# Normalising on two engines instead of three, new prices in the planner, one copy for the third bank of turned weights

## The chip, the core and the metric

The kernel runs on one core of a Trainium2 chip. The metric is the device time of one execution in microseconds, as the median of the runs shown. TensorE does the matrix products and the transposes; VectorE (DVE), ScalarE (ACT) and GpSimd (POOL) move results out of the PSUM banks, split numbers into high and low parts, and do the softmax; SyncE (SP) issues the DMAs. All arithmetic is in float32, and products are made from high and low parts in a rounded format (`fp32r`), so that one product of the reference is three matmuls.

## The reference

Three parts follow each other. Attention over 4 batches and 12 heads of 448 x 64; a feed-forward net with a gating convolution; and an attention with 4 experts, of which each row takes its best two.

```python
scores = scale * q @ k.T                      # (4, 12, 448, 448), causal
attn = exp(scores - max) / (sum + 1e-9)
x = attn @ v                                  # -> (4, 448, 768)

h = maximum(x @ w_in, 0.0)                    # 768 -> 1024
conv_out = sum over k of conv_w[k] * hp[:, k:k + S]   # 3 taps along the sequence
x = h * sigmoid(conv_out) @ w_out             # 1024 -> 768

topk = the two largest of x @ w_gate
for e in range(4):
    q, k, v = x @ wq[e], x @ wk[e], x @ wv[e] # 768 -> 64 each
    a = causal softmax of scale * q @ k.T
    ye = a @ v @ wo[e]                        # 64 -> 768
    out += weight of e (0 where not chosen) * ye
```

## The kernel before

Two heads, or two experts, make a **pair**: one takes the lower 64 partitions and the other the upper. There are 24 pairs of heads (6 in each batch) and 8 pairs of experts (2 in each batch), and all 32 go through the same steps. `scores` (L683) makes the causal scores of a pair, 24 matmuls into four banks (L734), DVE takes the masked maximum while copying them out (L711, tile `e`, with the maxima in `stat`), and ACT does the exponential with its sum (L715). `norms` (L748) adds the sums (L753), takes the reciprocal (L755) and multiplies the ten pieces of `e` with it: L760 on ACT, L763 on DVE or POOL. The pieces have 64, 192, 320 or 384 columns (four, two, two and two of them in a pair). For expert pairs L763 multiplies with the gate `coef` as well, and there ACT doesn't take part. `weigh` (L783) turns the weights: 14 transposes (L781) into banks, whose contents are copied into the tile `z` (by the helper `high`, L670 on ACT, L672 on DVE, L674 on POOL), and eight matmuls with the values (`rest`, L814). The first bank of transposes gives four small copies of 128 columns, two banks give one copy of 512 each, and the third gives two copies of 256. A subtraction (helper `low`, L678) gives the low part of a split number, on DVE or POOL.

The FFN works in eight slices of 128 of the 1024 columns: the weights are loaded and, in batch 0, split into tiles `slab` (`split_in`, L902); L966 makes the products; L984 is the ReLU on ACT, L990 to L1003 the convolution, L1010 the tanh. L885 to L889 are the rounding of numbers by integer steps in `single`. `output` (L1134) multiplies with the experts' output weights, copies a bank of 128 x 448 to the tile `work` and writes it out (L1155).

Nothing runs in the order of the text. Each step is recorded in `Plan` with the engines that may do it, a price for each, its inputs and outputs; `Plan.run` ranks the steps by how much work hangs on them, `schedule` hands each engine the ready step of the highest rank at the planned time, and then everything is written out in the order of planned starts. The prices are formulas (`scale_cost` for normalising, `psum_cost` for copies out of a bank, `LAG` for the time from the end of a step on one engine to the start of one that reads it on another), `SHIFTS` is a table that nudges ranks, and `FILLS` (30) idle products (L1160) may stand where TensorE has nothing to do. An engine executes its steps in the written order, and waits on semaphores for data. The choice of an engine for each step is the plan's too. So a step that takes longer than its price makes whatever was planned behind it late, and what stands behind that on the same engine.

## Time and profile before

| | us |
|---|---|
| median of 3 runs | 534.32 |
| lowest and highest | 533.75, 536.55 |
| the profiled execution | 535.11 |
| its span, first to last instruction | 533.3 |
| PE busy | 515.4 |
| DVE busy | 421.6 |
| ACT busy | 357.7 |
| POOL busy | 112.0 |

The profile comes from one execution. Its span leaves out some 2 us around the first and the last instruction. "Busy" is the time in which an instruction of that engine runs; waits are idle time in front of an instruction, and the profile names the instruction that ended them (the releaser). A line of a helper, like L670 or L678, stands for many different steps, which are told apart by the tiles that they read and write. PEclk is the granted clock of TensorE as a share of full speed.

### The profile page before, as it was taken

How to read it: one execution, taken by the hardware profiler on the slowest of the kernel's cores; microseconds unless marked ns; L12 is line 12 of the kernel's file. 1: busy time of each engine (PE TensorE's matmuls, PEld its weight loads, DVE VectorE, ACT ScalarE, POOL GpSimd, SP SyncE). 2: the span in 40 equal slices, each digit the busy share in tenths (PEclk: the TensorE clock that was granted, in tenths of full speed). 3: DMA queues.
4: the chain of work that ended last, by engine and by line, in shares of the span. 5: the costliest groups of instructions: out<-in, count | busy, mean ns of one | idle time of the engine just before them, and what ended most of it. 6: DMA issues, size and time to landing. Idle time of an engine off the chain costs nothing.

```text
span 533.3 us, 10436 instructions
## 1 busy us (share of the span) xinstructions
PE 515.4 (97%) x3554; PEld 436.2 (82%) x3556; DVE 421.6 (79%) x1300; ACT 357.7 (67%) x1058; POOL 112.0 (21%) x132
## 2 busy tenths in 40 slices
PE   8799999899899999899999999999999999999997
PEld 4678888778689898798898777998987778989875
DVE  6999599889798549999259999986389999842581
ACT  2876279789986557686249986755488867732572
POOL 3152017334232021160012511101114000000010
PEclk9999999899989999999999999999999999999999
DMA  9984246845587011374201573763003315610042
GB/s 239 256 222 135 63 149 195 255 120 206 167 246 201 23 36 37 139 250 163 68 2 46 146 219 84 249 215 87 1 1 113 117 49 194 221 59 1 10 154 104
DMA packets 63381, 69.92 MB, mean 131 GB/s; under 512 B 36576, under 2 KB 57312, under 8 KB 63328
## 3 DMA queue, kind: packets, MB, share of 16 engines
q1 hardware_dynamic: 63328, 69.26, 42.7%
q8 instruction: 28, 0.46, 0.4%
q14 instruction: 25, 0.20, 0.1%
HBM read 55.87 MB, written 13.37 MB: 130 GB/s over the span
## 4 chain that ended last, share of the span: by engine, by line
PE 47%; DVE 25%; ACT 8%; issue 2%; ACTq 0%; DVEq 0%
PE pf L966 34%; DVE e L711 7%; DVE e L763 5%; PE bank L814 5%; DVE z L672 4%; PE bank L781 3%; ACT e L715 3%; PE bank L734 3%; ACT e L760 2%; DVE pair L678 1%; DVE pair L672 1%; DVE work L995 1%; PE bank L966 1%; ACT z L670 1%; PE pf L1074 1%
## 5 line engine op out<-in xcount | busy, mean ns | idle before, releaser
L966 PE MATMUL pf<-pair,slab 128*128 128x448 f32 (+2 forms) x984 | 218.5, 368 | 4.3 <-ACT hp L984 2.7
L966 PEld LDWEIGHTS pf<-pair,slab 128*128 128x128 f32 x984 | 171.8, 189 | 22.2 <-ACT hp L984 3.7
L715 ACT ACTIVATE e<-e,stat 128x192 f32<-128x192 f32 (+3 forms) x256 | 127.1, 499 | 23.8 <-DVE stat L711 23.4
L711 DVE CUSTOM_DVE_ANT_0 e<-bank,mask 128x448 f32<-128x448 f32 (+3 forms) x256 | 92.1, 414 | 6.7 <-PE bank L734 6.5
L966 PE MATMUL pf<-pair,wqks 128*128 128x448 f32 x384 | 81.1, 369 | 0.0
L966 PEld LDWEIGHTS pf<-pair,wqks 128*128 128x128 f32 x384 | 71.4, 188 | 7.0 <-ACT pair L670 0.3
L781 PE MATMUL bank<-ident,e 128*128 128x128 f32 x448 | 70.7, 280 | 6.4 <-DVE stat L711 3.5
L678 POOL TENSOR_TENSOR pair<-work,pair 128x448 fp32r<-128x448 f32 (+1 forms) x39 | 48.6, 1260 | 105.6 <-PE bank L734 39.1
L781 PEld LDWEIGHTS bank<-ident,e 128*128 128x128 f32 x448 | 52.7, 142 | 16.9 <-DVE stat L711 3.6
L672 DVE COPY z<-bank 64x128 f32<-64x128 f32 (+2 forms) x121 | 48.7, 429 | 20.9 <-PE bank L781 16.7
L670 ACT ACTIVATE z<-bank 64x128 f32<-64x128 f32 (+2 forms) x135 | 45.8, 367 | 13.4 <-PE bank L814 7.4
L760 ACT ACTIVATE e<-e,stat 64x64 f32<-64x64 f32 (+3 forms) x116 | 49.4, 454 | 7.5 <-DVE stat L755 5.9
L734 PE MATMUL bank<-pair,pair 64*128 64x448 f32 (+3 forms) x576 | 49.6, 291 | 0.1
L814 PE MATMUL bank<-z,block 128*64 128x448 f32 (+3 forms) x384 | 48.7, 395 | 0.0
L715 ACT ACTIVATION_READ_ACCUMULATOR e<-e,stat 128x1 f32 (+1 forms) x256 | 48.5, 189 | 0.0
L995 DVE SCALAR_TENSOR_TENSOR work<-hp,cws,work 128x448 f32<-128x448 f32 x64 | 43.7, 694 | 3.9 <-ACT work L990 3.3
L734 PEld LDWEIGHTS bank<-pair,pair 64*128 64x128 f32 (+1 forms) x576 | 41.9, 172 | 3.3 <-issue 1.6
L814 PEld LDWEIGHTS bank<-z,block 128*64 128x64 f32 x384 | 27.3, 139 | 20.6 <-issue 11.5
L966 PE MATMUL pf<-wvs,pair 128*128 128x260 f32 x288 | 37.3, 286 | 0.0
L678 DVE TENSOR_TENSOR pair<-pf,pair 64x448 fp32r<-64x448 f32 (+1 forms) x24 | 15.0, 623 | 26.7 <-ACT pair L670 26.4
L966 PEld LDWEIGHTS pf<-wvs,pair 128*128 128x128 f32 x288 | 35.5, 188 | 0.3
L670 ACT ACTIVATE pair<-pf 64x448 fp32r<-64x448 f32 (+1 forms) x24 | 12.8, 541 | 32.3 <-PE pf L966 32.0
(99 smaller groups left out, 593.7 us busy)
## 6 DMA issues: line engine op xcount, KB each, us to landing
slab<-w_scratch SPq DMA_DIRECT2D x24, 768.0 KB, 4.6
work<-in_w_out SPq DMA_DIRECT2D x8, 768.0 KB, 4.8
work<-in_w_in SPq DMA_DIRECT2D x8, 768.0 KB, 5.7
w_scratch<-slab SPq DMA_DIRECT2D x8, 768.0 KB, 4.5
work<-in_qk SPq DMA_DIRECT2D x48, 112.0 KB, 3.4
work<-in_qk SPq DMA_DIRECT2D x24, 224.0 KB, 4.3
out<-work SPq DMA_DIRECT2D x24, 224.0 KB, 2.1
slab<-wo_scratch SPq DMA_DIRECT2D x6, 768.0 KB, 4.3
```

The costliest lines, as they stand in the source:

```text
L670: nc.scalar.activation(dst(), src(), AF.Copy)
L672: nc.vector.tensor_copy(dst(), src())
L678: return lambda e: engine(e).tensor_sub(dst(), src(), f32(h()))
L711: nc.vector.tensor_tensor_reduce(out=ec(o, c), in0=bank(o, c), in1=m, scale=-0.125, scalar=3.0e38, op0=OP.add, op1=OP.min, accum_out=st[ro ...
L715: nc.scalar.activation(ec(o, c), ec(o, c), AF.Exp, bias=st[rows, 0, o, c:c + 1], scale=-1.0, accum_out=st[rows, 1, o, c:c + 1])
L734: nc.tensor.matmul(bank(o, c), q(s)[own, Q0[c]:Q0[c] + QN[c]], k(t)[own, kc(o, c)], start=i == 0, stop=i == 2)
L760: nc.scalar.activation(dst(), src(), AF.Copy, scale=st[rows, 3, o, c:c + 1])
L763: engine(en).tensor_scalar(dst(), src(), st[rows, 3, o, c:c + 1], gate, op0=OP.mult, op1=OP.mult)
L781: P.op({"T": TURN}, lambda _: nc.tensor.transpose(dst(), src(), ident[:, :]), r=r, w=keys)
L814: nc.tensor.matmul(ps[own, S - n:S], v(k, o), z[:, 1024 * o + n0:1024 * o + n0 + n], start=k == 0, stop=k == 3)
L966: nc.tensor.matmul(out_ap(), a(), b(), start=first, stop=end), r=r, w=[(ps, 0)])
L995: return lambda _: nc.vector.scalar_tensor_tensor(cv[:, :S], hp[:, i:S + i], cws[:, fc, i:i + 1], cv[:, :S], op0=OP.mult, op1=OP.add)
```

## The change

1. Prices: normalising costs 0.053 us more on ACT, 0.05 on DVE, 0.055 on POOL; a copy of up to 128 columns out of a bank 0.065 more (0.12 below 64 columns); the lag between two steps on ACT is 0.15 instead of 0. The price of one FFN step on ACT is written out, so that it stays as it was.
2. `NORM` lets ACT and DVE normalise the pairs of heads, and DVE alone those of experts. POOL no longer does.
3. The third bank of transposes is copied in one step, which needs all four transposes. For that the columns of `z` are laid out in another order (`KEYS`).
4. The very last output is copied and written in two halves of 224 columns.
5. `SHIFTS` is another table (its rows tell nothing and are left out), and the plan comes out in another order.

```diff
-KEYS = ((0, 448), (448, 320), (832, 192), (768, 64))
+KEYS = ((0, 448), (704, 320), (512, 192), (448, 64))
...
 SHIFTS = (
-    (-1, 3596, 3648, -2), (15400, 386, 426, 0.5), (30038, 244, 284, 1), (-1, 4324, 4325, 0.5), (-1, 4323, 4324, 0.5),
+    (52200, 289, 299, 0.5), (-1, 4336, 4337, 2), (-1, 4333, 4334, -2), (-1, 4333, 4334, 2), (-1, 4331, 4332, -2),
...
-    LAG = {"TT": 0.0, "TA": 0.2, "TV": 0.2, "TG": 0.27, "TD": 0.19, "AT": 0.23, "AA": 0.0, "AV": 0.16, "AG": 0.17, "AD": 0.14,
+    LAG = {"TT": 0.0, "TA": 0.2, "TV": 0.2, "TG": 0.27, "TD": 0.19, "AT": 0.23, "AA": 0.15, "AV": 0.16, "AG": 0.17, "AD": 0.14,
...
+NORM = ("AV", "V")
...
 def scale_cost(n, on="AVG"):
-    return only(on, {"A": on_scalar(n) + 0.137, "V": on_vector2(n) + 0.065, "G": 0.245 + n * 0.000835})
+    return only(on, {"A": on_scalar(n) + 0.19, "V": on_vector2(n) + 0.115, "G": 0.3 + n * 0.000835})
...
 def psum_cost(n, on="A"):
-    return dict(only(on, {"A": on_scalar(n), "V": on_vector(n)}))
+    more = 0.12 if n < 64 else 0.065 if n <= 128 else 0.0
+    return dict(only(on, {"A": on_scalar(n) + more, "V": on_vector(n) + more}))
...
-            P.op(scale_cost(n, "VG" if moe else "AVG"), fn, r=r + [(st, "r")] + ([(COEF, b)] if moe else []), w=w)
+            P.op(scale_cost(n, NORM[moe]), fn, r=r + [(st, "r")] + ([(COEF, b)] if moe else []), w=w)
...
-            for o in range(2):
-                P.op(psum_cost(256, "AV"), high(lambda o=o: spread(z, 2048, 1024 * o + 64, 832, 128),
-                                                lambda t=t, o=o: t[:, 256 * o:256 * o + 256].rearrange("p (b c) -> p b c", b=2)),
-                     r=[(t, 2 * o), (t, 2 * o + 1)], w=[(z, (o, 3))])
+            P.op(psum_cost(512, "AV"), high(lambda: z[:, :].rearrange("p (a b) -> p a b", a=4)[:, :, 64:192],
+                                            lambda t=t: t[:, :].rearrange("p (a b) -> p a b", a=4)), r=[(t, j) for j in range(4)], w=[(z, 3)])
...
-        P.op({"T": 4 * 960 / 2400 + 0.23}, rest, r=[(z, (o, i)) for o in range(2) for i in range(4)] + v_r, w=[(ps, 0)], mode=2)
+        P.op({"T": 4 * 960 / 2400 + 0.23}, rest, r=[(z, (o, i)) for o in range(2) for i in range(3)] + [(z, 3)] + v_r, w=[(ps, 0)], mode=2)
...
-            P.op(scale_cost(S, "A"), c1, r=[(hp, 0), (CWS, 0)], w=[(cv, 0)])
+            P.op({"A": on_scalar(S) + 0.137}, c1, r=[(hp, 0), (CWS, 0)], w=[(cv, 0)])
...
-            P.op(psum_cost(S, "AV"), high(lambda o=o: o[:, :S], lambda ps=ps: ps[:, :S]), r=[(ps, 0)], w=[(o, 0)])
-            P.op(dma_cost(229376, 1792), lambda _, dc=dc, o=o: nc.sync.dma_start(out[b, dc], o[:, :S]), r=[(o, 0)])
+            parts = 1 + (b + 1 == B and dc + 1 == NK)
+            for i in range(parts):
+                own = slice(i * S // parts, (i + 1) * S // parts)
+                P.op(psum_cost(S // parts, "AV"), high(lambda o=o, own=own: o[:, own], lambda ps=ps, own=own: ps[:, own]), r=[(ps, 0)], w=[(o, i)])
+                P.op(dma_cost(229376 // parts, 1792 // parts), lambda _, dc=dc, o=o, own=own: nc.sync.dma_start(out[b, dc][:, own], o[:, own]), r=[(o, i)])
```

The instructions of each engine, counted in both programs: TensorE 3,338 in both, of the same kinds; DVE 1,302 before and 1,315 after; ACT 804 and 808; POOL 137 and 91; SP 264 and 265. The lines of the changed kernel are 16 to 19 higher than those of before (L763 is L781, L670 is L688, L678 is L696).

Three places of the order follow. The first is POOL in the middle of the program, around the first pairs of experts of batch 0 (`e_123`, `e_124`: the tiles of two such pairs; `pair`: a tile for a high or low part). Before:

```order
L678 TENSOR_TENSOR pair_139<-work_150,pair_136 128x448
L674 TENSOR_SCALAR pair_141<-work_150 128x896
L678 TENSOR_TENSOR pair_143<-work_150,pair_141 128x448 x2
L763 TENSOR_SCALAR e_123<-e_123,stat_86,coef 128x320
L763 TENSOR_SCALAR e_123<-e_123,stat_86,coef 128x192
L763 TENSOR_SCALAR e_123<-e_123,stat_86,coef 64x64
L763 TENSOR_SCALAR e_123<-e_123,stat_86,coef 128x384 x2
L763 TENSOR_SCALAR e_124<-e_124,stat_87,coef 64x64 x2
L674 TENSOR_SCALAR gx_146<-pair_138 128x128
```

The same pair on DVE after the change, whose POOL has no such step:

```order
L690 COPY z_114<-bank_157 128x4x128
L771 TENSOR_REDUCE stat_86<-stat_86 128x8
L773 RECIPROCAL stat_86<-stat_86 128x8
L781 TENSOR_SCALAR e_123<-e_123,stat_86,coef 128x320
L781 TENSOR_SCALAR e_123<-e_123,stat_86,coef 128x192 x2
L781 TENSOR_SCALAR e_123<-e_123,stat_86,coef 64x64 x2
L781 TENSOR_SCALAR e_123<-e_123,stat_86,coef 128x320
L781 TENSOR_SCALAR e_123<-e_123,stat_86,coef 64x64 x2
L781 TENSOR_SCALAR e_123<-e_123,stat_86,coef 128x384 x2
L696 TENSOR_TENSOR pair_131<-bank_156,pair_131 128x448
```

All ten pieces of this pair stand on DVE in one row now, where POOL had five of them.

The second place is ACT ahead of a ReLU (`hp`) of the FFN of batch 0, with the pieces of one pair of heads (`e_125`), turned weights (`z`) and a slab. Before:

```order
L760 ACTIVATE e_125<-e_125,stat_88 128x384
L1010 ACTIVATE work_150<-work_150 128x448
L670 ACTIVATE z_114<-bank_153 64x2x64
L670 ACTIVATE z_114<-bank_153 64x128
L670 ACTIVATE pair_142<-bank_155 128x448
L670 ACTIVATE z_114<-bank_153 64x128
L670 ACTIVATE z_114<-bank_157 128x2x256
L670 ACTIVATE z_114<-bank_153 64x2x64
L670 ACTIVATE z_114<-bank_156 128x2x256
L670 ACTIVATE slab_149<-work_150 128x768
L1010 ACTIVATE work_150<-work_150 128x448
L984 ACTIVATE hp_96<-pf_152 128x448
```

And the rows ahead of a ReLU of the same batch after the change:

```order
L778 ACTIVATE e_124<-e_124,stat_87 128x320
L778 ACTIVATE e_124<-e_124,stat_87 64x64 x2
L688 ACTIVATE z_114<-bank_158 128x4x128
L778 ACTIVATE e_124<-e_124,stat_87 128x192 x2
L778 ACTIVATE e_124<-e_124,stat_87 64x64 x2
L778 ACTIVATE e_124<-e_124,stat_87 128x384
L1026 ACTIVATE work_150<-work_150 128x448 x2
L733 ACTIVATE e_125,stat_88<-e_125,stat_88 128x448
L688 ACTIVATE pair_142<-work_150 128x896
L1000 ACTIVATE hp_95<-pf_152 128x448
```

The small copies out of a bank and the slab that stood ahead of the ReLU are elsewhere, and an exponential and a long pair copy stand there.

The third place is the end of DVE's program, with the last two pairs of experts (`e_123`, `e_124`). Before:

```order
L672 COPY work_150<-pf_151 128x448
L763 TENSOR_SCALAR e_123<-e_123,stat_86,coef 128x192
L763 TENSOR_SCALAR e_123<-e_123,stat_86,coef 64x64 x3
L763 TENSOR_SCALAR e_123<-e_123,stat_86,coef 128x384 x2
L753 TENSOR_REDUCE stat_87<-stat_87 128x8
```

After:

```order
L781 TENSOR_SCALAR e_123<-e_123,stat_87,coef 128x320
L781 TENSOR_SCALAR e_123<-e_123,stat_87,coef 64x64 x2
L781 TENSOR_SCALAR e_123<-e_123,stat_87,coef 128x320
L781 TENSOR_SCALAR e_123<-e_123,stat_87,coef 64x64 x2
L781 TENSOR_SCALAR e_123<-e_123,stat_87,coef 128x384
L771 TENSOR_REDUCE stat_88<-stat_88 128x8
L781 TENSOR_SCALAR e_123<-e_123,stat_87,coef 128x384
```

Before, the other four pieces of `e_123` were POOL's; now the last pair but one is wholly on DVE, two pieces of it further ahead than these rows.

## Rows read from the trace of the kernel before

**Rows 1.** The page, part 1: busy us (share of the span) xinstructions of each engine.
```profile
PE 515.4 (97%) x3554; PEld 436.2 (82%) x3556; DVE 421.6 (79%) x1300; ACT 357.7 (67%) x1058; POOL 112.0 (21%) x132
```

**Rows 2.** The page, part 4: shares of the span in the chain that ended last.
```profile
PE 47%; DVE 25%; ACT 8%; issue 2%; ACTq 0%; DVEq 0%
```

**Rows 3.** Busy by stage: us of PE, PEld, DVE, ACT, POOL; PEclk, DMA share, GB/s.
```profile
91.00:116.00 25.00, 23.39 (x178) 18.84 (x176) 21.42 (x68) 20.12 (x67) 10.38 (x11) 0.93 0.74 210
...
116.00:138.00 22.00, 21.06 (x133) 18.31 (x131) 20.39 (x52) 20.80 (x58) 9.60 (x8) 1.00 0.51 180
...
138.00:162.00 24.00, 22.18 (x135) 18.88 (x132) 21.50 (x45) 20.68 (x53) 5.11 (x7) 0.93 0.68 211
...
202.00:225.00 23.00, 21.62 (x180) 17.98 (x179) 22.06 (x75) 15.41 (x53) 3.05 (x5) 1.00 0.25 83
...
286.00:329.00 43.00, 41.81 (x350) 32.78 (x348) 40.64 (x166) 37.09 (x123) 13.54 (x17) 1.00 0.50 140
...
389.00:454.00 65.00, 63.46 (x493) 51.92 (x492) 61.62 (x224) 51.95 (x172) 10.31 (x15) 1.00 0.31 102
...
sum 533.30, PE 515.40 PEld 436.20 DVE 421.62 ACT 357.66 POOL 112.00; mean PE 36.81 PEld 31.16 DVE 30.12 ACT 25.55 POOL 8.00
```

**Rows 4.** The same view, two us at a time, behind two waits of TensorE.
```profile
102.00:104.00 2.00, 2.00 (x9) 1.91 (x10) 1.83 (x6) 0.95 (x2) 1.44 (x2) 0.51 1.01 366
...
104.00:106.00 2.00, 2.00 (x10) 1.75 (x9) 1.00 (x6) 2.00 (x8) 0.00 (x0) 0.63 1.09 214
...
146.00:148.00 2.00, 1.99 (x8) 1.08 (x9) 1.94 (x4) 1.97 (x5) 0.00 (x0) 0.61 0.64 259
...
148.00:150.00 2.00, 2.00 (x13) 1.73 (x10) 2.00 (x4) 1.50 (x6) 0.00 (x0) 0.54 0.64 191
```

**Rows 5.** Timeline, expert pairs: start us, us, engine line op tiles xcount [idle <-releaser].
```profile
211.79 3.15 POOL L763 TENSOR_SCALAR e<-e,stat,coef 128x320 f32<-128x320 f32 x5 [18.30 <-PE bank L781]
...
212.69 2.64 DVE L763 TENSOR_SCALAR e<-e,stat,coef 64x64 f32<-64x64 f32 x4
...
217.16 1.14 PE L781 MATMUL bank<-ident,e 128*128 128x128 f32 x8 [1.38 <-DVE stat L711]
...
435.71 3.13 DVE L763 TENSOR_SCALAR e<-e,stat,coef 128x320 f32<-128x320 f32 x9
```

**Rows 6.** The timeline around 97 to 102 us, DVE, POOL and PE.
```profile
97.48 3.22 DVE L763 TENSOR_SCALAR e<-e,stat 128x192 f32<-128x192 f32 x6
...
97.74 2.05 POOL L678 TENSOR_TENSOR slab<-work,slab 128x768 fp32r<-128x768 f32 x1 [0.29 <-ACT slab L670]
...
101.95 1.28 PE L781 MATMUL bank<-ident,e 128*128 128x128 f32 x5 [1.57 <-DVE pair L678]
```

**Rows 7.** The timeline around 136 to 145 us, ACT and PE.
```profile
135.94 4.07 ACT L760 ACTIVATE e<-e,stat 128x192 f32<-128x192 f32 x9
...
144.87 0.47 PE L966 MATMUL pf<-pair,slab 128*128 128x448 f32 x1 [1.80 <-ACT hp L984]
```

**Rows 8.** Groups of instructions, normalising: busy us, mean ns of one, idle before.
```profile
L763 DVE TENSOR_SCALAR e<-e,stat 64x64 f32<-64x64 f32 (+3 forms) x82 | 29.5, 387 | 1.7 <-ACT e L760 0.4
...
L763 DVE TENSOR_SCALAR e<-e,stat,coef 64x64 f32<-64x64 f32 (+3 forms) x69 | 24.8, 400 | 0.8
...
L763 POOL TENSOR_SCALAR e<-e,stat 64x64 f32<-64x64 f32 (+3 forms) x42 | 21.3, 516 | 61.4 <-DVE stat L755 34.1 <-ACT work L670 11.0 <-DVE e L763 7.5
...
L763 POOL TENSOR_SCALAR e<-e,stat,coef 64x64 f32<-64x64 f32 (+3 forms) x11 | 9.9, 904 | 67.6 <-ACT e L715 37.5 <-PE bank L781 18.3 <-DVE e L763 11.6
```

**Rows 9.** The same groups by form, copies of turned weights out of a bank.
```profile
L672 DVE COPY z<-bank 128x256 f32<-128x256 f32 x30 | 11.4, 413 | 5.5 <-PE bank L781 5.5
...
L672 DVE COPY z<-bank 128x512 f32<-128x512 f32 x34 | 22.8, 683 | 10.1 <-PE bank L781 6.4 <-PE bank L814 3.3
...
L670 ACT ACTIVATE z<-bank 128x256 f32<-128x256 f32 x34 | 11.7, 379 | 2.6 <-PE bank L781 2.3
```

**Rows 10.** The timeline at the end, ACT's last copy.
```profile
529.86 0.55 ACT L670 ACTIVATE work<-bank 128x448 f32<-128x448 f32 x1 [0.48 <-PE bank L966]
```

## What the change will do to the time

> **What bounds the kernel now.** I read the profile from the outside in. First the busy times: TensorE is busy for 97% of the span, DVE for 79%, ACT for 67%, POOL for 21% [rows 1]. The reader is to see that the time can fall only where TensorE waits or runs at its lower clock, since the change leaves its 3,338 instructions (matmuls, weight loads and the rest) the same in kind and number. Then the chain that ended last: it is 47% PE and 25% DVE [rows 2], so in a quarter of the span the releaser of TensorE's work is a queue of DVE. Then the busy time by stage, which says where the waits are [rows 3]: TensorE is busy 515.40 of 533.30 us, and of the 17.9 us in which it is idle 1.6 lie in 91 to 116, 0.9 in 116 to 138, 1.8 in 138 to 162, 1.4 in 202 to 225, 1.2 in 286 to 329 and 1.5 in 389 to 454; the stages left out between them have next to none, the two ends the rest. In two of these stages the granted clock is 0.93. [...]
>
> What makes these waits? The order was planned from prices, and where an engine takes longer than its price, TensorE arrives before its data. At 211.79 POOL normalises five pieces in 3.15 us, and beside it DVE takes 2.64 us for four small ones of 64x64 with the gate [rows 5]; undisturbed, nine of all sizes take 3.13 us at 435.71, 0.35 each [rows 5]. The old price of a 64x64 piece on DVE is 0.068 + 64/1920 + 0.065 = 0.17 us, four cost 0.7: DVE comes out 1.9 us late, and TensorE then waits 1.38 us for the masked maximum behind it. At 97.48 the same: six pieces take 3.22 us, 0.54 each, beside a subtraction of 2.05 us on POOL; TensorE waits 1.57 us at 101.95 for DVE [rows 6]. At 144.87 it waits 1.80 us for ACT's ReLU. ACT is late there without POOL: its nine pieces take 4.07 us [rows 7], where the old prices (0.187 + n/1200: 0.240, 0.347, 0.454 and 0.507 for 64, 192, 320 and 384, of which there are three, two, two and two) give 3.34.
>
> **The change, part by part.** *Prices.* The new ones add 0.053 to each piece on ACT and 0.05 on DVE, and 0.065 to each copy of up to 128 columns out of a bank: the nine pieces are now priced 3.81, and a 64x64 piece on DVE 0.22. They move towards the rows but do not reach them. A right price saves nothing by itself; it lets the plan put products in front of the work that would wait.
>
> *Normalising.* POOL loses 42 pieces without gate at 0.516 and 11 with gate at 0.904, 31 us; DVE gets 29 and 11 more, ACT 13 [rows 8]. On DVE's own rows (29.5 + 24.8 us for 151 pieces, 0.36 each) that is +14.4 us; on ACT, by the nine in 4.07, 0.45 each, +5.9. Against it stands what POOL cost DVE: 2.64 where four undisturbed pieces take 1.4, so 1.2 at this one place [rows 5], and 3.22 for 2.1, so 1.1, at the other [rows 6]; but there the neighbour is a subtraction, which POOL keeps (35 of this form become 31, six of slab form become four). At 211.6 the pair took DVE and POOL together until 215.3. All ten on DVE last 10 x 0.35 = 3.5 us and the copy of 0.68 us stands among them: 215.8, not earlier. So the gain is not that DVE is done sooner but that the plan knows when it is.
>
> [...]
>
> *Third bank.* DVE's 30 copies of 256 columns at 0.413 become 5 of 512 at 0.683: 12.4 - 3.4 = 9.0 us less [rows 9]. ACT's 34 at 0.379 become 27 longer ones; with DVE's ratio of the two kinds, 0.63 each, that is 4 us more for ACT, an estimate. The price of one copy is that the first half can't start after two transposes. Two more transposes are 0.5 us at most later (eight at 217.16 last 1.14, so 0.14 each, plus whatever product stands between), but one copy of 0.68 is shorter than two of 0.41 behind each other by 0.15: between -0.15 and +0.5 for the products that read it, hidden where other products stand in front. I take nothing, because in the order scores or products stand between the last transposes and the weighted sum in 25 of the 32 pairs before and in 24 now.
>
> *Other moves.* DVE also takes four more subtractions of pairs, two of slabs, two casts of slabs, and gives five z copies and some pair casts to ACT: with the above DVE gets +8.4 us in all by the trace's mean durations, ACT about +6, POOL loses about 31. Spread over 533 us DVE stays under 81%; what counts is where it falls. In the last pair before the end DVE gets four pieces more, 4 x 0.36 = 1.4 us [rows 8], and POOL's 2.3 us beside it go; seven idle products instead of three stand there in the order, and some 1.2 us of further products before the transposes. I take +0.3, from 0 to +1.4.
>
> *Last output in halves.* The last copy takes 0.55 us and starts at 529.86 [rows 10]; its transfer of 224 KB follows. Two copies of half length take at least 0.55 together, and by the mean of 0.379 for 256 columns on ACT [rows 9] about 0.75. So the second half is issued up to 0.2 later, behind the first, and carries half the bytes. Between -0.3 and +0.3, I take 0, as both copies are on the same engine.
>
> *New order.* Here lies the gain, place by place. At 217.16 the plan's error was 1.9 us and is now 10 x 0.35 less the new prices (four of 0.22, two each of 0.28, 0.35 and 0.38, 2.9) = 0.6: I take 1.1 of the 1.38 (0 to 1.4). At 101.95 the subtraction of POOL stays possible, so I take half of 3.3, 1.6 (0 to 3.3). At 144.87 ACT was late by 0.73 on the nine pieces, of which the new prices find 0.48, and the ten or so small z copies and the lag between ACT's own instructions (0 becomes 0.15) are priced now too: half of 3.5, 1.75 (0 to 3.5). The other middle waits (0.94 at 116 to 138, 1.5 at 389 to 454, about 1.2 between 286 and 329, 3.7 in all) have DVE or ACT as releaser too; by the same half, 1.8 (0 to 3.7). The added DVE load takes something back, where DVE has no room: it is busy 21.42 of 25 us, 20.39 of 22 and 61.62 of 65 in the stages around these waits [rows 3], a fifth of the kernel, and a fifth of 8.4 is 1.7 us (0 to 5).
>
> The sum: -1.1 - 1.6 - 1.75 - 1.8 + 1.7 + 0.3 = -4.3 us on the profiled 535.11, so 530.9. The profiled run lies 0.8 above the median of 534.32; against the median this is 530.0.
>
> **The rivals.** *No change.* The plan moves its mistakes elsewhere: the waits come back in other places because DVE now does what POOL did, and the 8.4 us arrive where it is the releaser (25% of the chain: 2.1 us), a new wait of 2 us eating the rest: 534. For it: prices that are still too low by about 0.05 a piece on 342 pieces. Against it: the two deepest waits have known causes that were repriced. [...]
>
> *Slower, by DVE between 91 and 138.* DVE is busy there 41.8 of 47 us, 5.2 to spare. In the new order one more pair of the second batch is normalised and copied in this stretch, beside the splitting of the FFN's weights. Its DVE work is 3.5 us at least (ten pieces); priced over all rows of both orders the 60 us of TensorE's work around it hold 59.6 us of DVE's before and 67.0 now, an estimate of 7.4 more. [...] It decides from 5.2 us of added work there. Against it: the same stretch loses POOL's interference, 1.1 us in the one case seen, and part of the added work stands behind products.
>
> *Everything goes.* Both deep waits vanish with their clock and the others with them: 1.4 + 3.3 + 3.5 + 3.7 = 11.9 less 1.5 of losses, 524.
>
> **How the numbers follow.** Forecast 0.42, everything goes 0.15, no change 0.24, slower 0.19. What a measurement here can tell is about 0.5%, 2.7 us: faster is under 531.6, slower over 537.0. The forecast's own range is 527 to 532.5, so a little of it is within 0.5%, and so is a little of the slower case: faster 0.55, same 0.29, slower 0.16. For 8 in 10 the range takes in the better part of the quick case, down to 524, and of the slow one, up to 538. The predicted time is 530.
>
> **What would show it.** The steps are right if in the profile after POOL is near 80 us and DVE near 425 or a little below 430 (+8.4 on 421.6, less some 4 us of interference, by the two places of 1.1 and 1.2), if PE's idle time falls from 17.9 to about 14, if the granted clock has at most one fall, and if the mean of DVE's normalising falls below 0.36. The third bank is right if the eight products behind it wait no more than before. The forecast is wrong if a new long wait of TensorE stands between 90 and 140 with DVE as releaser and a clock below 1 behind it; if PE's idle time falls but the time does not, the lower clock has taken the gain; and if the waits vanish by themselves at places whose engines were not repriced, the order did it and not the prices.

## The result and the profile after

The changed kernel takes 529.52 us (median of 6 runs, 528.43 to 531.82) against 535.06 for the kernel before (6 runs, 533.75 to 536.55): a ratio of 0.9902, with a 95% interval of 0.9874 to 0.993, so 3.7 to 6.7 us less. A second set of runs (**after_again** below, 12 beside 17 of the kernel before) gave 529.19 and 0.9927 (0.99 to 0.9953). The profiled execution took 528.43 us, with a span of 526.6.

The page's part 1 (busy us, share of the span, instructions) and part 4 (shares of the chain that ended last) of the changed kernel, against [rows 1] and [rows 2]:

```profile
PE 511.0 (97%) x3556; PEld 433.6 (82%) x3556; DVE 425.6 (81%) x1313; ACT 357.7 (68%) x1062; POOL 86.6 (16%) x86
...
PE 66%; DVE 27%; DMA 3%; ACT 2%; issue 1%; SPq 0%; ACTq 0%; DVEq 0%
```

TensorE's idle time, span less busy, goes from 533.3 - 515.4 = 17.9 us to 526.6 - 511.0 = 15.6. Its busy time goes down by 4.4 us as well, with the same matmuls. The two stretches of lower clock in the profile of before [rows 4] come to 1.7 + 1.7 = 3.4 us of that, and the stages below have none. So of 6.7 us between the two spans 2.3 are waits and 4.4 are busy time, most of it clock.

Busy time by stage of the changed kernel (us of PE, PEld, DVE, ACT, POOL; PEclk; DMA share; GB/s), against [rows 3]:

```profile
90.00:115.00 25.00, 24.90 (x216) 19.75 (x212) 24.14 (x73) 19.24 (x62) 6.32 (x6) 1.00 0.69 198
115.00:140.00 25.00, 23.89 (x153) 19.62 (x154) 24.94 (x62) 23.07 (x63) 8.59 (x5) 1.00 0.59 193
140.00:165.00 25.00, 24.58 (x154) 20.68 (x152) 24.67 (x71) 24.11 (x78) 13.54 (x15) 1.00 0.87 247
165.00:200.00 35.00, 33.17 (x253) 29.52 (x252) 21.48 (x68) 17.14 (x52) 3.08 (x3) 1.00 0.11 27
200.00:230.00 30.00, 30.00 (x195) 26.18 (x190) 27.09 (x88) 20.74 (x60) 2.15 (x3) 1.00 0.45 145
...
285.00:325.00 40.00, 38.29 (x326) 30.43 (x323) 38.85 (x147) 33.59 (x111) 9.79 (x9) 1.00 0.51 138
...
385.00:450.00 65.00, 64.39 (x504) 53.30 (x503) 58.62 (x213) 51.25 (x165) 8.51 (x10) 1.00 0.32 103
...
sum 526.60, PE 511.01 PEld 433.56 DVE 425.63 ACT 357.68 POOL 86.65; mean PE 36.50 PEld 30.97 DVE 30.40 ACT 25.55 POOL 6.19
```

The last stage of each kernel, first before, then after:

```profile
514.00:533.30 19.30, 14.81 (x88) 10.82 (x87) 6.10 (x15) 7.75 (x21) 0.00 (x0) 0.97 0.40 137
```

```profile
508.00:526.60 18.60, 15.16 (x94) 11.43 (x92) 6.24 (x15) 7.49 (x19) 0.00 (x0) 1.00 0.43 140
```

And normalising on DVE in the changed kernel, against [rows 8] (xcount | busy us, mean ns of one | idle before):

```profile
L781 DVE TENSOR_SCALAR e<-e,stat 64x64 f32<-64x64 f32 (+3 forms) x111 | 37.1, 373 | 1.4 <-ACT e L778 0.3
...
L781 DVE TENSOR_SCALAR e<-e,stat,coef 64x64 f32<-64x64 f32 (+3 forms) x80 | 27.6, 381 | 0.8
```

The three places of the prediction are empty of waits: nothing stands for 101.95 and 144.87, and the stage of the expert pairs, 200 to 230, has none. A wait of 0.99 us for ACT's ReLU at 127.98 is much like the one of 0.94 before (116 to 138 in [rows 3]). DVE is busy for 73.75 of the 75 us between 90 and 165. TensorE's longest wait in the middle stands right behind that, and it is new (timeline of the changed kernel: start us, us, engine, line, op, tiles, idle before and its releaser):

```profile
163.69 2.85 POOL L696 TENSOR_TENSOR pair<-work,pair 128x448 fp32r<-128x448 f32 x2
164.00 1.55 DVE L1019 SCALAR_TENSOR_TENSOR work<-work,hp 128x448 f32<-128x448 f32 x1
...
165.59 1.20 DVE L690 CAST pair<-work 128x448 fp32r<-128x448 f32 x1
...
166.84 1.49 PE L982 MATMUL pf<-pair,wqks 128*128 128x448 f32 x6 [1.83 <-DVE pair L690]
```

Two instructions of DVE last 1.55 and 1.20 us beside two subtractions of POOL. The same forms mostly take 0.62 and 0.39. The two subtractions suffer too: 2.85 us together, where two take 2.25 elsewhere (311.95, below).

### The profile page after: what moved, and what is told of

Same layout as the page of the kernel before. It is cut to its first block, busy times and chain, and to the rows that moved or that the text cites. A ratio compares the mean times of both kernels' runs of the same rounds, so it can differ in the third digit from the quotient of the medians.

```text
span 526.6 us, 10385 instructions
## 1 busy us (share of the span) xinstructions
PE 511.0 (97%) x3556; PEld 433.6 (82%) x3556; DVE 425.6 (81%) x1313; ACT 357.7 (68%) x1062; POOL 86.6 (16%) x86
## 4 chain that ended last, share of the span: by engine, by line
PE 66%; DVE 27%; DMA 3%; ACT 2%; issue 1%; SPq 0%; ACTq 0%; DVEq 0%
PE pf L982 45%; DVE e L729 7%; PE bank L830 6%; PE bank L799 6%; PE bank L752 6%; DVE e L781 5%; DVE pair L696 3%; DVE z L690 3%; DVE work L1011 2%; DMA block<-in_vv 2%; DVE pair L690 1%; PE pf L1179 1%; DMA work<-in_qk 1%; PE bank L982 1%; DVE work L905 1%
## 5 line engine op out<-in xcount | busy, mean ns | idle before, releaser
L733 ACT ACTIVATE e<-e,stat 128x320 f32<-128x320 f32 (+3 forms) x256 | 126.9, 499 | 21.4 <-DVE stat L729 20.9
L729 DVE CUSTOM_DVE_ANT_0 e<-bank,mask 64x64 f32<-64x64 f32 (+3 forms) x256 | 93.0, 413 | 14.8 <-PE bank L752 14.5
L688 ACT ACTIVATE z<-bank 128x512 f32<-128x512 f32 (+1 forms) x133 | 53.0, 420 | 14.3 <-PE bank L830 8.5
L696 POOL TENSOR_TENSOR pair<-work,pair 128x448 fp32r<-128x448 f32 (+1 forms) x35 | 46.3, 1343 | 86.5 <-PE pf L1090 29.8
L778 ACT ACTIVATE e<-e,stat 64x64 f32<-64x64 f32 (+3 forms) x129 | 51.9, 447 | 5.4 <-DVE stat L773 4.1
L690 DVE COPY z<-bank 64x128 f32<-64x128 f32 (+1 forms) x91 | 38.0, 434 | 20.7 <-PE bank L799 11.8
L830 PE MATMUL bank<-z,block 128*64 128x448 f32 (+3 forms) x384 | 46.8, 386 | 0.0
L982 PE MATMUL pf<-wvs,pair 128*128 128x260 f32 x288 | 39.5, 288 | 0.0
L781 DVE TENSOR_SCALAR e<-e,stat 64x64 f32<-64x64 f32 (+3 forms) x111 | 37.1, 373 | 1.4 <-ACT e L778 0.3
L692 POOL TENSOR_SCALAR pair<-work 128x896 fp32r<-128x896 f32 (+2 forms) x17 | 16.2, 951 | 134.0 <-DMA work<-in_qk 69.2
```

What stands on the lines that cost most here:

```text
L688: nc.scalar.activation(dst(), src(), AF.Copy)
L690: nc.vector.tensor_copy(dst(), src())
L696: return lambda e: engine(e).tensor_sub(dst(), src(), f32(h()))
L729: nc.vector.tensor_tensor_reduce(out=ec(o, c), in0=bank(o, c), in1=m, scale=-0.125, scalar=3.0e38, op0=OP.add, op1=OP.min, accum_out=st[ro ...
L733: nc.scalar.activation(ec(o, c), ec(o, c), AF.Exp, bias=st[rows, 0, o, c:c + 1], scale=-1.0, accum_out=st[rows, 1, o, c:c + 1])
L778: nc.scalar.activation(dst(), src(), AF.Copy, scale=st[rows, 3, o, c:c + 1])
```

## Experiments in which the order is kept

The planner makes a new order whenever a price or an engine changes, so a part of the change can't be undone in the planner without changing everything. In these runs the plan stays as it is, and only what is written out for a step differs. Ratios are to the kernel before on the same chip.

**b_norm**: the kernel before, POOL's 53 pieces on DVE at the same places.

```diff
-                    engine(en).tensor_scalar(dst(), src(), st[rows, 3, o, c:c + 1], gate, op0=OP.mult, op1=OP.mult)
+                    nc.vector.tensor_scalar(dst(), src(), st[rows, 3, o, c:c + 1], gate, op0=OP.mult, op1=OP.mult)
```

> The kernel before with its order kept, and the 53 normalising pieces that POOL had done at the same places on DVE (L763 always issues on VectorE). Theory 'order' (the gain of the change lies in the waits that the new order covers, not in the engine as such): DVE gets 53 x 0.36 = 19 us more and loses some 6 us of interference, so its busy time goes from 421.6 to about 434, POOL from 112 to about 81; at the wait near 217 DVE has all ten pieces, some 0.5 us later than before. The time stays between 533.5 and 540 (before is 535.1), no gain. Rival 'contention' (POOL's pieces as such cost the 5 us): 531 or less, with PE's wait near 217 gone. Rival 'third bank': no difference within 1 us.

544.58 us, ratio 1.0213 (1.0185 to 1.0242). Page part 1:

```profile
PE 518.3 (95%) x3556; PEld 436.6 (80%) x3556; DVE 432.9 (80%) x1353; ACT 358.3 (66%) x1058; POOL 83.8 (15%) x79
```

The longest group of TensorE's waits (us in total, times, longest us):

```profile
PE bank L781 <- DVE z L672: 5.6, 2, 3.8
```

The time is 11 us longer, which is worse than every theory expected. TensorE's idle time is 543.5 - 518.3 = 25.2 us instead of 17.9, and its busy time 2.9 us longer, at a mean clock of 0.989 against 0.992. In an order that was planned for POOL, normalising on DVE alone doesn't pay. "Contention" in its simple form, that POOL's pieces as such cost the 5 us, falls.

**a_pool**: the changed kernel, 53 pieces back on POOL, wherever its plan leaves POOL idle.

```diff
+        for o in order:
+            if o.norm and o.engine == "V" and quota[o.norm] and all(e <= o.start or s >= o.start + o.pool for s, e in taken):
+                quota[o.norm] -= 1
+                taken.append((o.start, o.start + o.pool))
+                o.engine = "G"
```

> The changed kernel with its order kept, and 53 of its pieces on DVE (42 without and 11 with the gate) put on POOL at the same places of the plan, where the plan leaves POOL idle. Theory 'order': DVE loses 19 us of its own work and gets back some 6 to 10 us by interference; POOL's pieces end later than DVE's would (0.52 and 0.90 us against 0.37), and the time is 529.5 to 533 (the changed kernel is 529.5). Rival 'contention': 532 to 535, with DVE's normalising of 64x64 beside POOL at 1 us or more each. Rival 'free help' (POOL does one-input work beside DVE at no cost to it): under 529.5, by up to 2 us.

527.56 us, ratio 0.9881 (0.9861 to 0.9902). Page part 1:

```profile
PE 511.1 (97%) x3556; PEld 434.8 (83%) x3556; DVE 413.7 (79%) x1260; ACT 356.8 (68%) x1062; POOL 121.2 (23%) x139
```

The stage that had the new wait, by windows:

```profile
165.00:200.00 35.00, 35.00 (x270) 30.51 (x269) 19.98 (x68) 18.34 (x57) 7.85 (x11) 1.00 0.12 28
```

Normalising by line (xcount | busy us, mean ns of one | idle before):

```profile
L790 DVE TENSOR_SCALAR e<-e,stat 64x64 f32<-64x64 f32 (+3 forms) x69 | 25.5, 398 | 2.2 <-ACT e L787 0.7 <-POOL e L790 0.5
...
L790 POOL TENSOR_SCALAR e<-e,stat 64x64 f32<-64x64 f32 (+3 forms) x42 | 26.2, 628 | 66.2 <-DVE stat L782 49.1 <-ACT pair L697 8.5 <-issue 2.5
```

That lies where the rival "free help" put it and not where the theory did, 1.6 to 2.0 us under the medians of the changed kernel in its own two sets of runs. All runs of a_pool (526.73 to 528.14) are under all of a_two (528.99 to 530.98), which is the changed kernel but for one copy, in the same set. DVE loses 12 us of busy time and the new wait near 167 is gone. TensorE has a new one of 1.1 us at 19.62, for POOL's own first piece. The pieces aren't the same ones that POOL had before, but the plan's idle places for them. So POOL was a help in both orders; the change gave it away and gained nevertheless.

**after_again** and **a_pool_late**: the changed kernel once more, and a_pool with pieces on POOL only from 32 us of the plan on (`if o.start > 32 and o.norm ...`).

> The changed kernel itself once more, beside the next ones, so that the comparison is on one chip. Both theories: ratio to the kernel before 0.990, 528 to 530.

> The changed kernel with its order kept and 53 pieces of normalising on POOL where the plan leaves it idle, as in the run a_pool (which came out at ratio 0.9881 and showed a wait of 1.09 us for POOL's first piece at 19.62 and a clock of 0.86 behind it), but only from 32 us of the plan on. Theory 'order' as amended (POOL's pieces take DVE's work away and cost it little; what decides is whether TensorE waits): the wait at 19.6 and the low clock behind it go, 525.5 to 527.5, and 1 to 3 us below the changed kernel on the same chip. Rival 'contention' (DVE loses beside POOL what it is relieved of): equal to the changed kernel within 0.7 us.

529.19 us, 0.9927 (0.99 to 0.9953), and 527.77 us, 0.9884 (0.9841 to 0.9927). Here both ran side by side: 1.4 us between the medians, with 12 runs from 527.16 to 531.43 against 6 from 526.12 to 528.43. The ratios to the kernel before overlap, but with a_pool the small gain is seen twice. The wait at 19.6 is gone, and the time is just above the 525.5 to 527.5 of the theory.

**b_third**: the kernel before, the third bank in one copy, written out where the later of its two copies stood.

```diff
...
+            both = high(lambda: z[:, :].rearrange("p (a b) -> p a b", a=4)[:, :, 64:192], lambda t=t: t[:, :].rearrange("p (a b) -> p a b", a=4))
+            seen = []
+            def later(e):
+                seen.append(e)
+                if len(seen) == 2:
+                    both(e)
...
-                P.op(psum_cost(256, "AV"), high(lambda o=o: spread(z, 2048, 1024 * o + 64, 832, 128),
+                P.op(psum_cost(256, "AV"), later, r=[(t, 2 * o), (t, 2 * o + 1)], w=[(z, (o, 3))])
```

> The kernel before with its order kept and the third bank of turned weights in one copy, at the place and on the engine of the later of its two copies. Theory 'order': DVE's 30 copies of 256 columns become some 15 of 512, and ACT's 34 some 17, so each loses 2 us or so of busy time, and the eight products behind them wait at most 0.15 us less each; 533.5 to 535.5 (before is 535.1). Rival 'third bank' (fewer copies are what shortened the queues of ACT and DVE): 531 to 533, with the wait for ACT's ReLU near 144.9 shorter by 1 us or more. Rival 'contention': no difference.

534.92 us, 1.0013 (0.9985 to 1.004): nothing, as the theory had it. (The columns of `z` are in the new order here too.)

**a_two**: the changed kernel, its one copy issued as two behind each other.

```diff
-            P.op(psum_cost(512, "AV"), high(lambda: z[:, :].rearrange("p (a b) -> p a b", a=4)[:, :, 64:192],
...
+            two = [high(lambda o=o: z[:, :].rearrange("p (a b) -> p a b", a=4)[:, 2 * o:2 * o + 2, 64:192],
+                        lambda t=t, o=o: t[:, 256 * o:256 * o + 256].rearrange("p (b c) -> p b c", b=2)) for o in range(2)]
+            P.op(psum_cost(512, "AV"), lambda e, two=two: [f(e) for f in two], r=[(t, j) for j in range(4)], w=[(z, 3)])
```

> The changed kernel with its order kept, and the one copy of the third bank issued as two copies of 256 columns behind each other on the same engine. DVE's five cost 5 x (2 x 0.413 - 0.683) = 0.7 us more and ACT's 27 cost 27 x (2 x 0.379 - 0.593) = 4.5 us more. Theory 'order': little of it is on the path, 529.5 to 531.5. Rival 'third bank': 532 to 535.

529.79 us, 0.9926 (0.9906 to 0.9946), where the changed kernel has 0.9902 and 0.9927: nothing again. Both copies still wait for all four transposes here, so this run tests their length, and b_third the two together. Neither shows the third bank on the path.

**a_whole**: the changed kernel with the last output in one copy and one transfer.

```diff
-                own = slice(i * S // parts, (i + 1) * S // parts)
+                all_ = slice(0, S)
...
+                P.op(psum_cost(S // parts, "AV"), high(lambda o=o: o[:, all_], lambda ps=ps: ps[:, all_]) if i + 1 == parts else lambda e: None, r=[(ps, 0)], w=[(o, i)])
...
```

> The changed kernel with its order kept and the last output in one copy and one transfer of 224 KB, at the place of the second half. All theories: the time from the end of the last product to the end of the span (3.2 to 3.6 us) differs from the changed kernel's by less than 0.3 us either way; a difference of over 0.5 us would make the halves a term of their own.

One run, 530.26 us. The last copies in the timelines, of the changed kernel and of this one:

```profile
523.20 0.60 ACT L688 ACTIVATE work<-bank 128x224 f32<-128x224 f32 x2 [0.47 <-PE bank L982]
```

```profile
524.99 0.54 ACT L688 ACTIVATE work<-bank 128x448 f32<-128x448 f32 x1 [0.49 <-PE bank L982]
```

From the start of that copy to the end of the span it is 526.62 - 523.20 = 3.4 us with halves and 528.46 - 524.99 = 3.5 without: in these two executions the halves are worth 0.05 us, if anything.

## Experiments without the table

With `SHIFTS` empty, the planner's own order is compared, without the search behind the table. Each of these is one order, in which a wait more or less is chance; so they bear only differences of some us.

```diff
-SHIFTS = (
...
+SHIFTS = ()
```

**b_notable**, **a_notable** (the kernels before and after without the table) and **a_oldprice_notable** (the one after, with the old prices of normalising, of copies out of a bank and of the lag on ACT):

> The kernel before with an empty table SHIFTS: old prices, POOL normalising, third bank in two copies, but the order that the planner finds by itself. Theory 'rules' (the better prices give the better order): 540 to 548, clearly slower than the changed kernel without its table. Rival 'table' (the gain of the change is in the new table alone): the same within 1 us as the changed kernel without its table.

> The changed kernel with an empty table SHIFTS: new prices, no normalising on POOL, third bank in one copy, halves, and the planner's own order. Theory 'rules': 3 us or more below the kernel before without its table, 534 to 542. Rival 'table': within 1 us of it, both 538 to 546.

> The changed kernel with an empty table SHIFTS and the old prices (normalising, copies out of a bank, the lag on ACT), to be read against the run a_notable (new prices, 540.4) and b_notable (the kernel before without its table, 542.6). Theory 'prices' (the right prices are what makes the better order without a table): 542 to 546. Rival 'third bank and normalising' (the prices do nothing): 539.5 to 541.5.

| | us | ratio to before |
|---|---|---|
| before, no table | 542.55 | 1.0177 (1.0127 to 1.0228) |
| after, no table, old prices | 544.45 | 1.0211 (1.017 to 1.0252) |
| after, no table | 540.35 | 1.0127 (1.0079 to 1.0175) |

The waits of TensorE for DVE's normalising (line 712 in these files), first with the old prices, then with the new:

```profile
PE bank L730 <- DVE e L712: 5.1, 5, 2.7
```

```profile
PE bank L730 <- DVE e L712: 1.8, 4, 1.0
```

TensorE's busy time in the three (before, after with the old prices, after; spans of 540.2, 542.6 and 537.9 us):

```profile
PE 515.4 (95%) x3556; PEld 433.3 (80%) x3556; DVE 416.3 (77%) x1309; ACT 356.7 (66%) x1055; POOL 112.1 (21%) x128
```

```profile
PE 517.6 (95%) x3555; PEld 435.6 (80%) x3556; DVE 435.3 (80%) x1348; ACT 356.2 (66%) x1033; POOL 80.1 (15%) x79
```

```profile
PE 517.5 (96%) x3556; PEld 437.5 (81%) x3556; DVE 429.3 (80%) x1331; ACT 352.6 (66%) x1038; POOL 92.8 (17%) x89
```

With the old prices the other parts of the change make the order no better (1.0211 against 1.0177), and with the new ones it is 4.1 us faster than with the old. TensorE's idle time is 24.8, 25.0 and 20.4 us; it is 4.6 us less with the new prices than with the old, and the waits above, for repriced pieces, are 3.3 us less, while others fall and rise. Between before and after without the tables there are 2.2 us, under the 3 of the theory "rules" and over the 1 of its rival "table". Either table then takes off some 9 us (1.0177 to 1 for before) to 11 (1.0127 to 0.9927 for after). So in these three orders the prices carried the gain, and they had to pay for the normalising on DVE first. That they would in other orders isn't shown, and how much of the tables' difference of 2 us is luck of the search is open.

## Experiments on POOL ahead of its plan

The waits that are left in the changed kernel led to the last question. At 310.45 DVE normalises six pieces (timeline of the changed kernel):

```profile
310.45 4.12 DVE L781 TENSOR_SCALAR e<-e,stat 128x192 f32<-128x192 f32 x6
310.71 1.15 POOL L692 TENSOR_SCALAR pair<-work 128x896 fp32r<-128x896 f32 x1 [7.96 <-DMA work<-in_qk]
...
311.95 2.25 POOL L696 TENSOR_TENSOR pair<-work,pair 128x448 fp32r<-128x448 f32 x2
...
314.62 0.33 PE L799 MATMUL bank<-ident,e 128*128 128x128 f32 x1 [0.46 <-DVE e L781]
...
317.20 0.77 PE L799 MATMUL bank<-ident,e 128*128 128x128 f32 x5 [1.02 <-DVE stat L729]
```

The planner never places such steps of DVE and POOL side by side: in `schedule` they carry a common mark (`port`), and none of them is planned to start before the last one is over. It had POOL's subtractions behind these pieces. But an order is written out for each engine by itself; POOL's step waits only for its data, and starts when that has arrived, here at 310.71 after 7.96 us of waiting for a DMA. **a_wait** makes each step of POOL wait for the last step of DVE with that mark that is planned ahead of it:

```diff
+        last = None
...
+            k = len(TC.nc.cur_bb.bb.instructions)
             o.fn(o.engine)
+            mine = TC.nc.cur_bb.bb.instructions[k:]
+            if o.engine == "V" and "V" in o.port:
+                last = mine[-1]
+            if o.engine == "G" and last is not None:
+                TC.add_manual_dep(mine[0], last.name, mybir.DependencyInfo(mybir.DependencyClass.Sync, mybir.DependencyReason.DATA), reason="plan")
```

> The changed kernel with its order and engines kept. The planner never puts a step of POOL beside one of DVE's steps that use the same port, but nothing holds POOL back from starting before its planned place; here each step of POOL also waits for the last such step of DVE that is planned ahead of it (17 of POOL's steps get a wait for DVE that they did not have). Theory 'POOL ahead of plan' (subtractions on POOL start early, collide with DVE's normalising and make it late, as the six pieces that last 4.12 us at 309.55 in a_pool_late): the sum of what DVE's instructions last beyond their median while POOL runs falls from 16.6 us to under 8, the waits of TensorE near 314.6 and 317 (0.5 and 1.0 us) go, and the time is 526 to 528 (the changed kernel is 529.2). Rival 'held back' (what POOL does later comes too late for TensorE): 529.5 or more, with new waits for POOL's pair or slab (L696). Rival 'order' alone (interference is too small to matter): within 0.7 us of the changed kernel.

521.78 us (520.37 to 522.62), ratio 0.978 (0.9744 to 0.9816): 12 us under the kernel before and some 7.5 under the changed one. Page part 1:

```profile
PE 510.0 (98%) x3555; PEld 435.4 (84%) x3556; DVE 416.6 (80%) x1313; ACT 357.3 (69%) x1062; POOL 79.3 (15%) x86
```

Two stages by windows:

```profile
165.00:200.00 35.00, 35.00 (x271) 31.27 (x268) 21.16 (x80) 18.44 (x59) 4.08 (x4) 1.00 0.13 32
...
285.00:325.00 40.00, 39.69 (x333) 32.47 (x330) 38.61 (x151) 35.72 (x118) 7.59 (x8) 1.00 0.57 162
```

Normalising without the gate, by line:

```profile
L790 DVE TENSOR_SCALAR e<-e,stat 64x64 f32<-64x64 f32 (+3 forms) x111 | 32.6, 333 | 1.4 <-ACT e L787 0.3
```

The same six pieces, in the timeline:

```profile
305.75 1.67 DVE L790 TENSOR_SCALAR e<-e,stat 128x192 f32<-128x192 f32 x6
...
307.56 0.94 POOL L701 TENSOR_SCALAR pair<-work 128x896 fp32r<-128x896 f32 x1 [9.51 <-DMA block<-in_vv]
308.58 2.26 POOL L705 TENSOR_TENSOR pair<-work,pair 128x448 fp32r<-128x448 f32 x2
```

The six pieces take 1.67 us instead of 4.12, and the waits behind them, 0.5 and 1.0 us, are gone, as is the one near 167. TensorE's idle time is 519.2 - 510.0 = 9.2 us instead of 15.6, of which the start and the end of the kernel hold most: 4.7 lie before 30 us, and 3.5 behind the last product. The busy time of the two engines falls with the same instructions: DVE is busy for 416.6 us instead of 425.6, POOL for 79.3 instead of 86.6. Summed over DVE's instructions that run beside one of POOL, what they last beyond the median of their line, tiles and form falls from 13.5 us to 3.7 (14.0 in the kernel before). By this sum the expectation's 16.6 is 13.5. "Held back" falls but for one wait at the start: 1.9 us for POOL's pair at 14.99 (1.2 in the changed kernel). The gain is 7.5 us and not the 1 to 3 of the expectation, which had priced the visible waits of two places; the 6.4 us of idle time that went are the better measure, and how they are spread over the other places was not followed up.

**a_pool_wait**: a_pool_late with the same waits.

> The run a_pool_late (53 pieces back on POOL, ratio 0.9884, 527.8) with the same added waits of POOL for DVE. Theory 'POOL ahead of plan': both gains add, 524.5 to 526.5. Rival 'held back': 528 or more, since POOL's pieces then wait behind DVE's and TensorE behind them.

522.25 us, 0.9794 (0.976 to 0.9828). Page part 1:

```profile
PE 508.7 (98%) x3555; PEld 433.8 (83%) x3556; DVE 407.3 (78%) x1260; ACT 357.5 (69%) x1062; POOL 118.2 (23%) x139
```

The time is below what either theory expected, but no better than a_wait: the gains don't add. DVE is busy 9 us less than in a_wait, and the time is the same: in these orders, with POOL held to the plan, that much of DVE's load isn't what TensorE waits for. It may be that the gain of a_pool came from the one collision near 167 that was gone there; no run shows that by itself. The best kernel of this study is a_wait, whose interval lies below those of both kernels; a_pool_wait isn't apart from it.

## Why the prediction came out right

The forecast was 530.0, a gain of 4.3 us; measured are 529.52 and 5.5 us between the medians. By its own steps:

- **Waits of TensorE.** Without the clock, the sum lets 4.6 us of waits go (1.1, half of 1.57 and of 1.80, and 1.8) and has 1.7 + 0.3 come back: 2.6 net. Measured are 2.3 in all (17.9 to 15.6), and 2.7 in the middle: of 8.5 us in the six stages of [rows 3] 5.8 are left in those of after shown above (0.10 + 1.11 + 0.42 + 1.83 + 0 + 1.71 + 0.61 = 5.8). The net was right; the sign "about 14" was not what its own sum gave, and wasn't met. The three named places are empty. The wait at 166.84 is new, and those for the ReLU and of 285 to 325 stayed. That half of each would go was a guess more than a mechanism, and that the whole came out right is in part luck.
- **Clock.** The two falls were priced at 3.4 us, and half of that was taken. The terms of 3.3 and 3.5 us for the two deep waits hold 1.7 us of lower clock each, by [rows 4], but that a wait brings such a fall no run shows: the falls stood behind waits of 1.57 and 1.80 us [rows 6, 7], while the clock was 1.00 behind the 1.38 us at 217.16 before [rows 3] and behind the 1.83 us at 166.84 after. The profile after has none, so against the profiled run of before all went: of the 6.7 us between the spans 3.4 are the clock, where the forecast had 1.7 of 4.3. But before doesn't always have the falls. In its three sets of runs (17, 17 and 11) the executions with a mean clock of 0.998 or more have medians of 533.2, 531.7 and 531.2 us, and those with 0.995 or less 535.4, 536.4 and 535.5: 2.2 to 4.7 us apart. The changed kernel has lost the deep ones (0.997 at the lowest in the 12 runs of after_again, 0.996 in the six first), and its ten runs at 0.998 or more have a median of 529.2, 2.5 us under the 531.7 beside them. So in that set some half of the 4.4 us is the clock, and the total of the forecast is closer than its terms.
- **Prices.** The new order carries the gain: the third bank and the halves are worth nothing and normalising on DVE costs time where the order is kept. That the prices made the order better is supported by one order each (4.1 us), and not shown apart from the search behind the table.
- **Normalising.** DVE's busy time was to be 425 to 430 and is 425.6; the mean of its 191 pieces (37.1 + 27.6 us) is 0.34 us, under 0.36. POOL was to be near 80 and is 86.6; the same instructions take 79.3 in a_wait, so the rest is what POOL itself loses beside DVE. The step also counted some 4 us of interference as gone, and that was wrong: over DVE's instructions it is 13.5 us, after 14.0. The pieces went and the subtractions found other neighbours. The prediction had the evidence in hand, a subtraction beside six pieces in [rows 6], said that POOL keeps it, and still gave the credit. Its "four small ones of 64x64" at 212.69 [rows 5] are three and one of 128x192 (a row that joins several instructions shows the form of the first), and of the 2.64 us one piece has 1.48, which starts while POOL runs and ends 0.05 us behind POOL's last piece. And POOL's pieces were worth more than the rates say: doing them on DVE is 11 us dearer in the old order (b_norm), and putting pieces back on POOL is not dearer in the new one (a_pool).
- **Third bank, halves, end.** Taken as 0, 0 and +0.3: 0 by b_third and a_two; 0.05 us by the two last copies; at the end, 18.60 - 15.16 = 3.4 us idle in the last stage against 19.30 - 14.81 = 4.5 before, with four more idle products that count as busy. Behind the last product 3.5 us stand in both.
- **Rival "no change".** POOL was slower at the pieces: means of 516 against 387 ns and 904 against 400 in [rows 8], 628 against 398 in a_pool. They still were help there: without them the old order takes 11 us more (b_norm), and with them the new one 1.6 to 2.0 us less (a_pool). So moving them off POOL gave something away, but the rival's time didn't come, since the new order gave more. The 904 ns of [rows 8] for the gated pieces comes largely from one instruction of 4.23 us (226.51, below); their median is 0.61 us, against 0.38 on DVE. And the pieces on ACT, DVE and POOL are 320, not 342.
- **Rival "slower".** Its mechanism was there: DVE was busy for 98% of 90 to 165. TensorE still waited only 1.6 us there and 1.83 behind it, and the clock stayed at 1.00. The stage was as full as feared, and the plan had put enough products in front.

What the prediction missed altogether is behind the largest gain of these runs: waits that right prices can't remove, because the delay isn't in the price of a step but in a neighbour that starts ahead of plan (7.5 us in a_wait).

## What to carry to other kernels

Where a plan keeps steps of two engines apart, look in the trace whether the engines keep to it: a written order binds each engine to itself only, and an early start on an idle engine held up the busy one here (six pieces took 4.12 us for 1.67). Here the dependencies that enforce the plan cost one wait of 1.9 us at the start and gave back far more. And before crediting a change with removing interference, list which pairs of instructions collide and which of them the change takes away.

## What the runs showed of the hardware

The normalising pieces on DVE that started in the changed kernel while a longer instruction of POOL was running didn't get slower by one share (they took 2.2 to 3.9 times the median of their form); they ended shortly after POOL's instruction did. In the group at 310.45 the piece of 384 columns that starts at 310.98 ends at 312.08, 0.22 us behind the end of POOL's cast (310.71 + 1.15), and the next ones end at 313.19 and 314.41, 0.1 and 0.2 us behind the ends of POOL's two subtractions (311.95 + 1.13 and 313.04 + 1.16). Each row here joins two pieces, and its end is that of the second:

```profile
310.98 2.21 DVE L781 TENSOR_SCALAR e<-e,stat 128x384 f32<-128x384 f32 x2
...
311.95 1.13 POOL L696 TENSOR_TENSOR pair<-work,pair 128x448 fp32r<-128x448 f32 x1
...
312.00 2.41 DVE L781 TENSOR_SCALAR e<-e,stat 128x192 f32<-128x192 f32 x2
```

In a_wait the same pieces take 0.32 to 0.42 us. Over the whole profile of the changed kernel, seven such pieces start beside an instruction of POOL that outlasts their usual time, and all seven end behind it, by 0.11 to 0.22 us. The masked maximum, which reads a PSUM bank, wasn't touched: beside the cast and the subtractions in a_wait it takes 0.61 and 0.48 us, as elsewhere, and 70 of its instructions that start beside POOL in the changed kernel last 0.1 us more than their medians, all together.

```profile
307.87 0.61 DVE L738 CUSTOM_DVE_ANT_0 e<-bank,mask 128x448 f32<-128x448 f32 x1
...
308.42 0.48 DVE L738 CUSTOM_DVE_ANT_0 e<-bank,mask 128x320 f32<-128x320 f32 x1
...
308.58 1.15 POOL L705 TENSOR_TENSOR pair<-work,pair 128x448 fp32r<-128x448 f32 x1
```

It went the other way as well. In the kernel before, a piece of 64x64 on POOL that starts while DVE runs one takes 4.23 us, where the next takes 0.39: DVE executes eight more steps on `work`, `hp` and `pair` (no bank) without a gap, and POOL's piece ends 0.1 us behind the last of them (229.96 + 0.68).

```profile
226.51 4.23 POOL L763 TENSOR_SCALAR e<-e,stat,coef 64x64 f32<-64x64 f32 x1 [11.57 <-DVE e L763]
...
229.96 0.68 DVE L995 SCALAR_TENSOR_TENSOR work<-hp,cws,work 128x448 f32<-128x448 f32 x1
```

Other steps of DVE lasted longer beside POOL too: the step with two inputs at 164.00 took 1.55 us, and the cast at 165.59 1.20, where the medians of their forms are 0.62 and 0.39 in the same profile. By what the two engines hold each other up, no row shows. No instruction of POOL reads a PSUM bank in the profiles of before, after and a_wait (132, 86 and 86 instructions); the copies out of banks are ACT's and DVE's alone.

The lower clock came and went between executions of one program: of the kernel before, the six first executions beside b_norm had mean clocks of 1.0, 1.0, 0.994, 1.0, 0.994 and 1.0.
